# Moving the later loads of a transformer-block backward kernel from the Pool queue to the SP queue

## The chip, the cores and the metric

One core of one Trainium2 chip. The metric is the device time of one execution in microseconds (us). Quoted times are medians of 3 to 7 executions. All executions used below are of the same, undisturbed state except where it is said. The profiled execution has a span about 2 us shorter than its time; spans are compared with spans and times with times. "Granted PE clock" is the share of the matmul engine's full clock that the profile shows as granted, as a mean over the span or a stretch.

The engines appear under the profile's names: PE (matmul), PEld (its weight loads), DVE (vector), ACT (scalar), POOL (GpSimd), SP (sync; here it only issues transfers). Sixteen DMA engines serve all queues of the core.

## The reference

Forward and gradients of `x + attention(layernorm(x)) + ffn(layernorm(x))` for a decode step: batch 4, one query position, D = 512, 32 query heads on 8 key/value heads of 128, a cache of 4096 positions of which only the last 1024 are attended, and a gated FFN of width 1792. Cut to what matters:

```python
def _A_ref(x, k_cache, v_cache, wq, wo):        # W = 1024 of Sk = 4096
    k = jnp.repeat(k_cache[:, :, Sk - W:, :], rep, axis=1)
    v = jnp.repeat(v_cache[:, :, Sk - W:, :], rep, axis=1)
    ...
return x + _A_ref(xn, ...) + _B_ref(xn, ...)
# outputs: the value, and d/d(x, k_cache, v_cache, wq, wo, w_gate, w_up, w_down)
```

The gradients of both caches are outputs in full size. Three quarters of each are zeros, which must still be written: 50 MB of the 81 MB that the kernel writes.

## The kernel before

After the FFN part, four groups (t = 0 to 3, two key/value heads each) pass through the same steps. Group t + 2 is fetched when group t no longer needs its buffers. Everything fetched after the start is issued by `nc.gpsimd` (POOL); all results are stored by `nc.sync` (SP); the zero fills are issued by `nc.scalar` (ACT).

```python
def load_w(t):
    eng = nc.gpsimd if t else nc.sync
    pool = wpool[t % 2]
    wo_t[t] = pool.tile([P, HG, D], BF16, name="wo_sb", tag="wo")
    eng.dma_start(out=wo_t[t][:], in_=wo_v[t])
    wq_t[t] = pool.tile([P, ND, CW], BF16, name="wq_sb", tag="wq")
    eng.dma_start(out=wq_t[t][:], in_=wq_v[t])

def load_kv(t, k, g):
    d_, src, nm = ((k_t, A_k_cache, "kb"), (v_t, A_v_cache, "vb"))[k]
    tl = kvpool[(GP * t + g) % (2 * GP)].tile([P, J, Dh], BF16, name=nm, tag=nm)
    (nc.gpsimd if GP * t + g > GP else nc.sync).dma_start(out=tl[...], in_=src[...])
    ...
def load_next(t):
    if t + 2 < NT:
        load_w(t + 2)
        for k in range(2):
            for g in range(GP):
                load_kv(t + 2, k, g)
...
def zeros(n):                      # n units of 768 KB, at most 4 in one transfer
    ...
        w = min(n, B * G - r, GP * 2)
        z = store(nc.scalar, zdst, zsrc, "zeros", ["rest", "zeros"])
...
# how many units to fill at the four places of each group's score step
ZN = ((0, 4, 4, 4), (0, 4, 4, 2), (2, 4, 4, 4), (4, 4, 4, 4))
```

A scheduler places the issues, so their order on an engine is not always that of the text. And every transfer issued by SP or ACT takes one of eight completion semaphores in turn; an issue waits until the transfer eight places before it has landed. The transfers of POOL have eight of their own. Below, the transfer that took a semaphore last is called its holder.

## Time and profile before

| | before |
|---|---|
| time, median of 3 (range) | 281.89 us (280.82 to 281.97) |
| profiled span, granted PE clock | 279.6 us, 0.888 |
| PE, DVE, ACT, POOL busy | 76%, 57%, 41%, 20% |
| bytes moved by the queues, mean rate over the span | 112.15 MB, 401 GB/s |

No compute engine is near full, and the transfers are: the prediction shows the lines. Two more views of the kernel before are needed for what follows. First, stretches of the windows view (columns: stretch, length; busy us and count for PE, PEld, DVE, ACT, POOL; PE clock; mean busy share of the DMA engines; GB/s), cut where the kernel after will differ:

```profile
100.00:120.00 20.00, 19.13 (x223) 11.12 (x220) 13.42 (x25) 11.26 (x20) 4.64 (x7) 0.91 1.01 419
150.00:170.00 20.00, 16.56 (x222) 10.95 (x221) 11.51 (x20) 9.96 (x18) 7.46 (x10) 1.00 0.99 381
215.00:220.00 5.00, 4.12 (x40) 2.45 (x40) 2.72 (x7) 2.18 (x6) 0.00 (x0) 1.00 1.00 424
```

Second, the last stretches, in the same columns:

```profile
266.00:270.00 4.00, 0.00 (x0) 0.00 (x0) 2.27 (x7) 0.00 (x0) 0.00 (x0) 0.50 1.01 407
270.00:274.00 4.00, 0.00 (x0) 0.00 (x0) 0.00 (x0) 0.00 (x0) 0.00 (x0) 0.50 0.29 114
274.00:278.00 4.00, 0.00 (x0) 0.00 (x0) 0.00 (x0) 0.00 (x0) 0.00 (x0) 0.50 0.06 25
```

The last column but one is the thing to read. From 274 to 278 us the mean share is 0.06, one sixteenth: 25 GB/s, as if one of sixteen engines still had work and fifteen had none. The others ran out between 270 and 273 us.

### The profile page before, as it was taken

What the parts mean: (1) busy time and instruction counts of PE and PEld (TensorE: products, weight loads), DVE (VectorE), ACT (ScalarE), POOL (GpSimd) and SP (SyncE); (2) the same over time, 40 slices, a digit from 0 to 9 for tenths busy, and PEclk for the clock granted to TensorE, in tenths of its full rate; (3) what the DMA queues carried; (4) which work ended last, traced back from release to release, by engine and by line L of the source; (5) the groups of instructions that cost most, each with busy time, mean ns of one, the idle gap of its engine ahead of it and who ended that gap; (6) DMA issues with size and microseconds to landing.
All of it is one profiled execution on the core that took longest, in us unless ns stands there. A gap on an engine that the chain in (4) does not pass through costs nothing.

```text
span 279.6 us, 7185 instructions
## 1 busy us (share of the span) xinstructions
PE 212.1 (76%) x3126; PEld 137.7 (49%) x3132; DVE 158.7 (57%) x336; ACT 115.0 (41%) x214; POOL 56.0 (20%) x56
## 2 busy tenths in 40 slices
PE   1978976988769879968797978699897775689400
PEld 0856854744435565535465745356664442355200
DVE  6955644546357657654665555477654634376530
ACT  1331643444335246636253544373444442525400
POOL 3890003040200345020007600200520020020000
PEclk9985998699797997999689999999999997597955
DMA  7999999999999999999999999999999999999970
GB/s 236 446 392 430 425 403 392 414 411 423 425 426 422 422 423 416 417 432 423 427 418 350 387 407 430 421 425 421 425 415 431 428 422 423 425 432 421 422 311 22
DMA packets 19423, 112.15 MB, mean 401 GB/s; under 512 B 1456, under 2 KB 5056, under 8 KB 10432
## 3 DMA queue, kind: packets, MB, share of 16 engines
q10 hardware_dynamic: 4400, 50.34, 42.7%
q1 hardware_dynamic: 12304, 44.58, 39.3%
q0 software_dynamic: 2688, 16.78, 15.0%
q8 instruction: 24, 0.39, 0.5%
q14 instruction: 7, 0.06, 0.0%
HBM read 30.68 MB, written 81.01 MB: 399 GB/s over the span
## 4 chain that ended last, share of the span: by engine, by line
PE 52%; DVE 19%; DMA 18%; issue 3%; POOL 2%; ACT 2%; ACTq 0%; DVEq 0%
DMA out_dram<-osb_q 13%; PE T_ps L402 9%; PE kv_ps L540 8%; DVE T_sb L101 6%; PE S_ps L407 6%; DMA out_dram<-osb_g 5%; PE woT_ps L339 3%; PE wgT_ps L745 3%; PE acc_ps L213 2%; PE wqT_ps L598 2%; PE dwo_ps L559 2%; POOL P_x L420 2%; PE od_ps L512 2%; PE dwg_ps L718 2%; PE do_ps L344 2%
## 5 line engine op out<-in xcount | busy, mean ns | idle before, releaser
L101 DVE COPY T_sb<-T_ps 128x1024 bf16<-128x1024 bf16 x64 | 43.8, 690 | 40.1 <-PE T_ps L402 39.6
L99 ACT CAST stg_dv<-kv_ps 128x512 bf16<-128x512 f32 x57 | 30.1, 594 | 33.5 <-PE kv_ps L540 25.8
L99 ACT CAST stg_dk<-kv_ps 128x512 bf16<-128x512 f32 x40 | 22.3, 592 | 36.4 <-PE kv_ps L540 22.8
L540 PE MATMUL kv_ps<-domr,P_x 128*128 128x512 bf16 x63 | 23.4, 439 | 10.5 <-ACT stg_dv L99 5.1
L387 POOL TENSOR_TENSOR domr<-r,msk 128x512 bf16<-128x512 bf16 x8 | 8.2, 1040 | 74.1 <-DVE r L380 74.1
L99 ACT CAST osb_g<-dwg_ps 128x512 bf16<-128x512 f32 (+1 forms) x28 | 14.2, 538 | 19.0 <-PE dwg_ps L718 9.2
L402 PE MATMUL T_ps<-ident,kb 128*128 128x128 bf16 x256 | 21.9, 222 | 0.0
L402 PEld LDWEIGHTS <-kb 128*128 128x128 bf16 x256 | 17.1, 100 | 8.6 <-issue 5.7
L540 PE MATMUL kv_ps<-qmr,dS_x 128*128 128x512 bf16 x60 | 20.9, 432 | 0.5 <-DVE stg_dk L101 0.2
L402 PE MATMUL T_ps<-ident,vb 128*128 128x128 bf16 x256 | 20.8, 223 | 0.1
L99 ACT CAST osb_o<-dwo_ps 128x512 bf16<-128x512 f32 x25 | 14.6, 586 | 12.9 <-PE dwo_ps L559 11.8
L402 PEld LDWEIGHTS <-vb 128*128 128x128 bf16 x256 | 16.2, 100 | 6.9 <-issue 5.0
L407 PE MATMUL S_ps<-T_sb,dom 128*32 128x256 bf16 x128 | 12.7, 387 | 8.3 <-DVE T_sb L101 7.8
L420 POOL TENSOR_TENSOR P_x<-P_b,bmsk 128x1024 bf16<-128x1024 bf16 x4 | 7.6, 1893 | 56.2 <-ACT P_b L468 56.2
L99 ACT CAST osb_q<-dwq_ps 128x512 bf16<-128x512 f32 x25 | 14.1, 589 | 11.1 <-PE dwq_ps L571 6.1
L101 DVE CAST stg_dk<-kv_ps 128x512 bf16<-128x512 f32 x24 | 16.0, 684 | 1.8 <-PE kv_ps L540 1.7
L101 DVE COPY woT<-woT_ps 128x1024 bf16<-128x1024 bf16 x16 | 11.0, 689 | 10.0 <-PE woT_ps L339 10.0
L407 PE MATMUL S_ps<-T_sb,qm 128*32 128x256 bf16 x128 | 13.1, 388 | 4.0 <-DVE T_sb L101 4.0
L339 PE MATMUL woT_ps<-ident,wo_sb 128*128 128x128 bf16 x128 | 12.3, 248 | 2.7 <-DVE stg_dv L101 1.9
L101 DVE COPY wgT<-wgT_ps 128x1024 bf16<-128x1024 bf16 x14 | 9.7, 692 | 7.6 <-PE wgT_ps L745 7.6
L339 PEld LDWEIGHTS <-wo_sb 128*128 128x128 bf16 x128 | 10.4, 113 | 7.2 <-issue 6.4
L101 DVE COPY wqT<-wqT_ps 128x1024 bf16<-128x1024 bf16 x16 | 11.0, 687 | 4.7 <-PE wqT_ps L598 4.6
(214 smaller groups left out, 397.4 us busy)
## 6 DMA issues: line engine op xcount, KB each, us to landing
out_dram<-ztile ACTq DMA_DIRECT2D x14, 3072.0 KB, 22.4
out_dram<-stg_dv SPq DMA_DIRECT2D x8, 1024.0 KB, 25.4
out_dram<-stg_dk SPq DMA_DIRECT2D x8, 1024.0 KB, 17.2
out_dram<-ztile ACTq DMA_DIRECT2D x4, 1536.0 KB, 12.7
kb<-in_A_k_cache_dram POOLq DMA_DIRECT2D x5, 1024.0 KB, 20.0
vb<-in_A_v_cache_dram POOLq DMA_DIRECT2D x5, 1024.0 KB, 24.3
out_dram<-osb_o SPq DMA_DIRECT2D x8, 512.0 KB, 15.8
out_dram<-osb_q SPq DMA_DIRECT2D x8, 512.0 KB, 28.1
```

The source lines that it names most:

```text
L99: last.append(nc.scalar.copy(out=out, in_=in_))
L101: return nc.vector.tensor_copy(out=out, in_=in_)
L213: nc.tensor.matmul(ps[:, c, :], lhsT=lf(c), rhs=rhs, start=(k == 0), stop=(k == len(terms) - 1))
L339: nc.tensor.transpose(wT_ps[:, i, c, :], wo_sb[:, 2 * h2 + i, c * P:(c + 1) * P], ident[:])
L344: nc.tensor.matmul(do_ps[i * RG:(i + 1) * RG, 2 * h2:2 * h2 + 2], lhsT=dyT8[:, c, :], rhs=woT[:, :, c, :].rearrange("p j (g x) -> p j g x" ...
L387: nc.gpsimd.tensor_tensor(out=mr[:, g], in0=st[t]["r4"][:, k, :].unsqueeze(1).broadcast_to([P, NQ, Dh]), in1=msk[:, :, g].unsqueeze(2).bro ...
L402: nc.tensor.transpose(T_ps[:, jj, :], blks[(t, g)][:, q * JQ + jj, :], ident[:])
L407: nc.tensor.matmul(ps[b * RG:(b + 1) * RG, :], lhsT=lf[:, b, s * RG:(s + 1) * RG], rhs=T_sb[:, :, b], start=(g == 0 and q == 0), stop=(g = ...
L420: eng.tensor_tensor(out=dst[:].rearrange("p j (m b) -> p (j m) b", b=B), in0=src[:].unsqueeze(2).broadcast_to([P, WQ, B]), in1=bmsk[:].uns ...
L512: nc.tensor.matmul(od_ps[r0:r0 + rep * B, 0, :], lhsT=pT[:, j % JQ, (j // JQ) * GP + g:P:NS], rhs=blks[(t, g)][:, j, :], start=(j == 0), s ...
L540: nc.tensor.matmul(mps[:].rearrange("p q d -> p (q d)"), lhsT=src[:, jj, :], rhs=mr[:, g].rearrange("p q d -> p (q d)"), start=True, stop= ...
L745: nc.tensor.transpose(wT_ps[:, i, c, :], wsb[:, c, fc * P:(fc + 1) * P], ident[:])
```

## The change

The intent: take the 16 later loads (16.78 MB) from POOL's queue and put them into SP's, between the stores; the weights when a group ends, keys and values one at a time in the next group's key steps.

```diff
-    def load_w(t):
-        eng = nc.gpsimd if t else nc.sync
+    loads = deque()
+    def pull(n):
+        for _ in range(min(n, len(loads))):
+            loads.popleft()()
+    def fetch(out, in_, first):
+        d = (nc.sync if first else nc.sync).dma_start(out=out, in_=in_)
+    def load_w(t, k):
         ...                               # wo if k == 0, else wq, each through fetch
     def load_kv(t, k, g):
-        (nc.gpsimd if GP * t + g > GP else nc.sync).dma_start(out=..., in_=...)
+        fetch(..., ..., GP * t + g <= GP)
     def load_next(t):
         if t + 2 < NT:
-            load_w(t + 2)
+            for k in range(2):
+                load_w(t + 2, k)
             for k in range(2):
                 for g in range(GP):
-                    load_kv(t + 2, k, g)
+                    loads.append(lambda k=k, g=g: load_kv(t + 2, k, g))
 ...                                       # in the score step, q counts the blocks
                 tick(2 if k or q % 2 else 1)
+                if k == 0 and q % 2 == 0:
+                    pull(1)
 ...                                       # before the groups
-        load_w(1)
-        for k in range(2):
-            load_kv(1, k, 1)
+        for k in range(2):
+            loads.append(lambda k=k: load_w(1, k))
+        for k in range(2):
+            loads.append(lambda k=k: load_kv(1, k, 1))
```

(Cuts marked with dots.) In the built programs PE, DVE and ACT have the same instructions in the same order before and after. SP's stream has the 16 loads more, POOL's 16 fewer. The scheduler puts group 1's four loads ahead of all eight stores of the FFN weight gradients (`osb_g`), although the text defers them.

More of the change, by code (lines that the diff above doesn't have):

```diff
@@ L275 @@
     kvpool = [kvp] * 3
-    def load_w(t):
-        eng = nc.gpsimd if t else nc.sync
-        pool = wpool[t % 2]
-        wo_t[t] = pool.tile([P, HG, D], BF16, name="wo_sb", tag="wo")
-        eng.dma_start(out=wo_t[t][:], in_=wo_v[t])
-        wq_t[t] = pool.tile([P, ND, CW], BF16, name="wq_sb", tag="wq")
-        eng.dma_start(out=wq_t[t][:], in_=wq_v[t])
+    loads = deque()
[5 more added lines that the diff above has]
+    def load_w(t, k):
+        pool = wpool[t % 2]
+        if k == 0:
+            wo_t[t] = pool.tile([P, HG, D], BF16, name="wo_sb", tag="wo")
+            fetch(wo_t[t][:], wo_v[t], t == 0)
+        else:
+            wq_t[t] = pool.tile([P, ND, CW], BF16, name="wq_sb", tag="wq")
+            fetch(wq_t[t][:], wq_v[t], t == 0)
     def load_kv(t, k, g):
@@ L287, in load_kv @@
         tl = kvpool[(GP * t + g) % (2 * GP)].tile([P, J, Dh], BF16, name=nm, tag=nm)
-        (nc.gpsimd if GP * t + g > GP else nc.sync).dma_start(out=tl[:].rearrange("p j d -> p (j d)"),
-                          in_=src[:, t * GP + g, K0:Sk, :].rearrange("b (m j) d -> m b (j d)", j=J))
+        fetch(tl[:].rearrange("p j d -> p (j d)"),
+             src[:, t * GP + g, K0:Sk, :].rearrange("b (m j) d -> m b (j d)", j=J), GP * t + g <= GP)
         d_[(t, g)] = tl
@@ L613 @@
     NF4 = (NF + 3) // 4
-    load_w(0)
+    for k in range(2):
+        load_w(0, k)
     for k in range(2):
```

## The prediction

> **What bounds the kernel now.** I read the page's DMA rows first, because every engine on the page is well below full (PE 76%, DVE 57%, ACT 41%) while the DMA row is not.
>
> ```profile
> DMA  7999999999999999999999999999999999999970
> GB/s 236 446 392 430 425 403 392 414 411 423 425 426 422 422 423 416 417 432 423 427 418 350 387 407 430 421 425 421 425 415 431 428 422 423 425 432 421 422 311 22
> q10 hardware_dynamic: 4400, 50.34, 42.7%
> q1 hardware_dynamic: 12304, 44.58, 39.3%
> q0 software_dynamic: 2688, 16.78, 15.0%
> ```
>
> The 16 DMA engines are 90% busy or more in 37 of 40 slices. q10 is the zero fill issued by ACT, q1 is SP (first loads, all stores of results), q0 is Pool's loads: 16 of 1 MB, 16.78 MB. Bytes over busy time give the rate of each: q10 50.34 MB in 0.427 x 279.6 us = 422 GB/s, q1 406 GB/s, q0 400 GB/s. So the kernel moves 112 MB at a nearly fixed rate, and what can be won is only the places where the rate drops. The windows view sizes them (columns: stretch, length, then busy us and count of PE, PEld, DVE, ACT, POOL, then PE clock, DMA share, GB/s):
>
> ```profile
> 5.00:40.00 35.00, 28.73 (x541) 23.47 (x542) 23.21 (x71) 12.77 (x20) 12.59 (x8) 0.85 1.03 421
> 40.00:75.00 35.00, 28.28 (x361) 18.18 (x363) 17.86 (x35) 14.64 (x31) 8.54 (x9) 0.88 1.02 408
> 75.00:150.00 75.00, 63.97 (x975) 40.17 (x977) 45.19 (x88) 33.31 (x63) 13.32 (x15) 0.90 1.01 423
> 150.00:157.00 7.00, 5.54 (x104) 4.29 (x104) 3.54 (x7) 3.71 (x7) 3.55 (x6) 1.00 0.95 322
> 157.00:165.00 8.00, 7.10 (x77) 4.27 (x76) 5.32 (x9) 4.10 (x7) 3.91 (x6) 1.00 1.01 405
> 165.00:271.00 106.00, 78.31 (x1071) 47.24 (x1072) 60.30 (x117) 45.21 (x86) 11.61 (x8) 0.91 1.01 422
> 271.00:279.60 8.60, 0.00 (x0) 0.00 (x0) 0.00 (x0) 0.00 (x0) 0.00 (x0) 0.50 0.09 34
> ```
>
> Three dips, all where Pool's loads run. Then the chain that ended last, and the waits, to see where DMA holds the compute:
>
> ```profile
> 56.90 13.97 DMA out_dram<-osb_g
> 226.83 35.79 DMA out_dram<-osb_q
> ACT osb_g L99 <- DMA out_dram<-osb_g: 7.0, 4, 3.6
> ```
>
> The chain is compute up to 57 us, one wait for a store of an FFN gradient tile to land (its buffer is reused), compute again from 71 to 227, and from there the DMA queue itself. Last, the DMA view of the stretch 44 to 56 us, for how three queues share:
>
> ```profile
> q10 hardware_dynamic: 253, 2.97, 62.4%
> q0 software_dynamic: 252, 1.49, 29.7%
> q1 hardware_dynamic: 335, 0.34, 7.9%
> ```
>
> q10 and q0 moved the same number of packets (253 and 252) but twice the bytes, and the store queue, whose rows are 1 to 3.5 KB there, got a fourteenth of the bytes. The queues take turns by packet, so a queue's share of the rate follows its row size.
>
> **What the Trainium skill says.** (1) "DMA: Bandwidth & Descriptors", section "Issuing engines are not separate DMA queues": all issuers share the same 16 engines, and issuing from several only saves sequencer time. The trace agrees as to the rate: 421 GB/s with SP alone (5 to 40 us, almost all q1), 422 with SP and ACT (165 to 271). (2) Same page, "Queues, rings and completion order": each engine goes round the queues packet by packet. The 253 to 252 packets agree. (3) Same page, "Where 436 GB/s comes from": a ceiling of 435 GB/s. The trace sits at 421 to 423, so there is no higher rate waiting. (4) Same page, "Latency and other measured facts": first byte after some 0.6 us for SP and ACT, 1 us for Pool. No line here shows the first byte of one transfer; the landing times (10 to 43 us) are queueing.
>
> **The change part by part.** The listing of the two built programs shows that PE, DVE and ACT run the same instructions in the same order; only SP's stream, Pool's stream and semaphore waits differ.
>
> (a) It removes 16 DMA issues from Pool, 0.53 to 0.77 us each, about 9.5 us of 56 us busy. Pool is 20% busy and 2% of the chain: worth about 0, at most 0.6 us per group where the product od_x stood behind a load (97.79 in the timeline, after the issue at 97.18).
>
> (b) It adds 16 issues of some 0.55 us to SP, about 9 us. SP waits for results nearly all the time: worth 0 unless a load that waits for its buffer holds up a finished store.
>
> (c) The 16.78 MB leave q0 for q1. If the dips are the cost of the software queue, they are recovered: 40 to 75 us, (421 - 408) x 35 = 0.46 MB or 1.1 us at 421; 150 to 157, (423 - 322) x 7 = 0.71 MB or 1.7 us; 157 to 165, 17 x 8 = 0.14 MB or 0.3 us. Sum 3.1 us, 1.1% of 281.9. The other reckoning, q0 at 422 in place of 400, gives 16.78 MB x (1/400 - 1/422) = 2.2 us. That is the whole of what can be won from rate.
>
> (d) Group 1's four loads (4 MB) go into SP's queue at about 44 us, ahead of the eight osb_g stores. Estimate: the 3 MB zero fill on q10 runs till about 52 us with the last 1 KB-row osb_d stores trickling beside it; then SP has the engines alone, 4 MB / 0.42 = 9.8 us, till 62; the first osb_g lands at about 63 us (before, 61.9) and the next ones at 64, 66 and 66 to 70 (before 65.5, 71.0, 76.1), as the ACT waits ended then. So the first release comes 1 us later, the others 1 to 6 us earlier. PE had about 4 us idle between 55 and 75 us; I take a shift of the compute of -1 us, between -3 and +2.
>
> (e) At 150 us the queue runs dry (322 GB/s, q10 has nothing left). Before, Pool issues V at 149.98 and K at 152.44 as soon as group 1 has done with its buffers. In the new SP stream only V stands there; both K loads come behind the weights, which wait for the sums at 156.5, and behind the second dK store at 158. So from about 149 to 157 only V and one dK store are there, 2 MB, against 2.25 MB that moved from 150 to 157 before. Whatever (c) gained up to then (1.1 us) only makes the queue run dry sooner; when it refills is set by compute. In time: the refill comes about 1.5 us after 157, when the old kernel would be 0.25 MB + 1.5 us x 0.42 = 0.9 MB further, that is 2 us; with the 0.3 us of 157 to 165 got back, +1.7 us; with the compute shift of (d), -1, about +0.7 us. If instead the compute before 150 us comes 2 to 3 us sooner, the dip closes and the change wins 1 to 2 us.
>
> (f) All transfers of SP and ACT take completion semaphores in turn from one set of eight, each waiting for its last holder; the Pool loads had eight of their own. With 16 more in the one set, an issue waits for the transfer eight places back. In the listing most of those are 20 us or more old; a few zero fills on ACT wait for a load issued 10 to 16 us before (at 121, 173 and 181 us). One or two such waits of 1 to 3 us on ACT, whose compute has slack there: 0 to +1.5 us.
>
> Sum: (c) up to -3.1, (e) taking most of it back, (d) -1 to +1, (f) +0.5: I put -0.5 us.
>
> **The rivals.** *A: the rate is recovered whole.* Software loads are slow (packets of q0 were 51.9% of the engines' time in 150 to 157 for 1.02 MB, 281 GB/s), and the hardware queue fills the dip. For it: all three dips stand on Pool's loads. Against: 75 to 150 us had six of those loads and ran at 423. Result 279 us. *B: the dip at 150 grows*, as compute, not the queue, refills it and K comes later. For it: the order of SP's stream, and q10 empty from 150 to 157. Against: dK or compute may come sooner. Result 282 to 284. *C: head of line.* A load waiting for its buffer blocks stores; or stores and loads in one queue behind zero fills with larger rows land late, and a group's PE waits for weights or K. For it: loads now share q1's part with stores. Against: group 2's weights are issued at 104 us and needed at 134, K and V at 157, and even five MB at 8 KB rows against 12 KB rows (0.4 of 422, 170 GB/s) take under 30 us, and the zeros do not last that long. Result 285 to 290. *D: nothing*, since queueing hides every issue: 281.9.
>
> **Range and chances.** The middle of A, B and D lies at 281.4 us. A and the best of (d) bound it below at 278.8, B with a semaphore wait above at 284.6. Faster by over 2% needs 5.6 us; the dips hold only 3.1, so that takes a second gain I don't see: 0.03. Slower by over 2% is C: 0.09. Within 2%: 0.88.
>
> **What would show it.** q0 is gone from the queue rows, q1 holds 61 MB; the rate in 5 to 40 and after 165 us stays 420 to 424; 44 to 63 us has the loads on q1 and no dip; the ACT wait for osb_g ends near 63 us and later ones are shorter; a dip at or just before 150 us stays, with q10 empty, at least as deep; DMA ends some 8 us before the span does, as before. I am wrong if PE waits for woT, K or V at a group's start, if SP's waits on a load's buffer delay a finished store by many us, if there is no dip at 150 us, or if the steady rate itself moves off 422.

## The result

| | before | after |
|---|---|---|
| time, median of 4 runs each (range) | 281.93 us (280.82 to 282.18) | 285.04 us (284.37 to 286.31) |
| ratio after/before, 95% interval | | 1.0123 (1.0079 to 1.0168) |
| profiled span, PE clock | 279.6 us, 0.888 | 284.2 us, 0.891 |

A ratio is the mean time of one kernel's fast runs over that of the other's fast runs of the same rounds, so it is not quite the ratio of the medians. The change costs about 3 us: within 2%, but 0.4 us above the predicted range, whose middle lay 0.5 us below the kernel before. The profiled execution of the kernel after was the slowest of its four (286.31 us), so its span, 4.6 us longer than before, overstates the change by about 1.5 us.

The kernel after, the page's rate row in 40 slices and its queue rows:

```profile
GB/s 239 442 398 426 423 395 428 385 394 373 421 419 424 422 381 386 320 427 426 428 414 394 328 314 422 430 424 425 427 410 289 419 434 408 422 421 425 423 417 182
q1 hardware_dynamic: 15760, 61.35, 55.0%
q10 hardware_dynamic: 4400, 50.34, 42.0%
```

The software queue is gone, as wanted, and no rate was won. Bytes over busy time give SP's queue 61.35 MB in 0.550 x 284.2 us, 393 GB/s; before, the same bytes on q1 and q0 took 0.543 x 279.6 us, 404 GB/s. The rate row of before had one deep dip, 350; the row of after has 320, 328, 314 and 289. Sized by the windows view of the kernel after:

```profile
5.00:40.00 35.00, 28.37 (x554) 23.36 (x555) 23.15 (x72) 12.78 (x20) 12.57 (x8) 0.85 1.02 418
40.00:75.00 35.00, 23.10 (x316) 14.54 (x316) 14.79 (x31) 12.59 (x26) 4.04 (x4) 0.85 1.00 396
100.00:120.00 20.00, 16.68 (x216) 10.23 (x206) 11.56 (x21) 9.90 (x18) 5.41 (x5) 0.91 0.99 359
150.00:170.00 20.00, 17.36 (x362) 12.36 (x361) 12.56 (x26) 8.43 (x16) 5.93 (x5) 1.00 0.93 337
215.00:220.00 5.00, 4.71 (x94) 3.80 (x92) 2.77 (x8) 2.17 (x4) 1.64 (x2) 0.88 0.59 246
278.00:284.20 6.20, 0.00 (x0) 0.00 (x0) 0.00 (x0) 0.00 (x0) 0.00 (x0) 0.50 0.38 147
```

Against before (408, 419, 381 and 424 in the four middle stretches), the bytes missing are worth, at 423 GB/s, (408 - 396) x 35 / 423 = 1.0 us, then 2.8, 2.1 and 2.1 us: 8 us of missing work. ("Missing work" is time that the missing bytes would take at the steady rate.) The span grew by 4.6 us only. Two questions follow: what makes the holes, and where did half of their cost go?

**The first hole** starts at 44 us. SP's timeline before, and then after (start, duration, engine, line, transfer):

```profile
43.23 0.37 SPq L105 DMA_DIRECT2D out_dram<-osb_d  x1
46.30 32.69 SPq L105 DMA_DIRECT2D out_dram<-osb_g  x8
```

```profile
42.87 0.37 SPq L105 DMA_DIRECT2D out_dram<-osb_d  x1
43.33 1.25 SPq L284 DMA_DIRECT2D wo_sb<-in_A_wo_dram  x1
44.76 1.13 SPq L284 DMA_DIRECT2D wq_sb<-in_A_wq_dram  x1
45.99 1.44 SPq L284 DMA_DIRECT2D kb<-in_A_k_cache_dram  x1
47.48 1.72 SPq L284 DMA_DIRECT2D vb<-in_A_v_cache_dram  x1
49.31 33.88 SPq L105 DMA_DIRECT2D out_dram<-osb_g  x8
```

Four loads of 1 MB stand before the first `osb_g` store, which goes out 3 us later and, behind their bytes, lands later still. The chain of waits of the kernel after (start, duration, what) and ACT's waits (us in total, times, longest):

```profile
49.31 17.65 DMA out_dram<-osb_g
...
163.77 31.45 DMA kb<-in_A_k_cache_dram
195.24 0.61 ACTq L105
```

```profile
ACT osb_g L99 <- DMA out_dram<-osb_g: 9.8, 1, 9.8
ACT stg_dv L99 <- DMA kb<-in_A_k_cache_dram: 5.9, 1, 5.9
ACT P_b L481 <- DMA out_dram<-stg_dk: 3.6, 1, 3.6
```

The first release shows on ACT's timeline, where the bracket is the idle time before and what ended it; before, and then after:

```profile
61.94 0.59 ACT L99 CAST osb_g<-dwg_ps 128x512 bf16<-128x512 f32 x1 [0.83 <-DMA out_dram<-osb_g]
```

```profile
67.06 0.58 ACT L99 CAST osb_g<-dwg_ps 128x512 bf16<-128x512 f32 x1 [9.76 <-DMA out_dram<-osb_g]
```

So the first `osb_g` lands at 67 us instead of 62, and PE is idle from 60 to 65 us. The row product that ends group 0's attention (`od_r` on DVE) starts at 96.04 us before and at 100.33 us after: the compute runs 4.3 us late, while the queue drains at its own pace. So the queue is thin at 100 to 120 us, and again when group 1 ends, at 150 to 170 us.

Thin is not empty: the share of DMA in these two stretches is 0.99 and 0.93, so the engines were mostly busy and their packets took longer. From 116 to 118 us, for example, the DMA view counts 152 packets of 2.2 KB on average at a share of 0.87; that is 0.87 x 16 x 2 us / 152 = 183 ns each, where 423 GB/s over 16 engines would give 82 ns. Only at 215 to 220 us (share 0.59, 246 of 424 GB/s) did the engines stand idle in proportion to the missing bytes. In what follows a "hole" is a stretch with bytes missing, of either kind; why a packet takes longer when little else is queued, no run tests.

**The last hole** comes from elsewhere. ACT waits 5.9 us before a copy of value gradients, for a key load that this copy does not need. What stands in between is the zero fill that ACT issues at 195.24 us: its completion semaphore was last held by that key load, which took 31.45 us to land. The 3.6 us wait, at the fill of 181.13 us, is of the same kind. (Two such waits exist before too, 4.4 and 3.4 us, but late, at 234 and 239 us.) They hold up the casts that PE waits for: `od_r` of group 2 starts at 209.95 us after, at 196.96 us before, 13 us late where group 1's was 5 us late (153.96 against 148.78). The next zero fills are placed in group 3's steps; they go out at 220.58 and 228.33 us instead of 206.51 and 213.80, and the queue is nearly dry at 218 us (share 0.44 from 217 to 219 us).

**The end.** In the kernel after, the last stretches read

```profile
274.00:278.00 4.00, 0.00 (x0) 0.00 (x0) 0.13 (x1) 0.00 (x0) 0.00 (x0) 0.50 0.99 407
278.00:282.00 4.00, 0.00 (x0) 0.00 (x0) 0.00 (x0) 0.00 (x0) 0.00 (x0) 0.50 0.58 224
282.00:284.00 2.00, 0.00 (x0) 0.00 (x0) 0.00 (x0) 0.00 (x0) 0.00 (x0) 0.50 0.02 8
```

There is no long 0.06 tail any more: all engines run dry nearly together. That is my theory of where half the cost went. One DMA engine lags behind the others; before, it works without a pause until 278 us while the others wait at the end. Every hole lets it catch up, and until it has, holes are free. This is an inference from mean shares, and how far it holds is taken up at the end.

### The profile page after: what moved, and what is told of

Same layout as the page of the kernel before. It is cut to its first block, busy times and chain, and to the rows that moved or that the text cites.

```text
span 284.2 us, 7178 instructions
## 1 busy us (share of the span) xinstructions
PE 210.4 (74%) x3126; PEld 136.6 (48%) x3132; DVE 158.3 (56%) x336; ACT 115.0 (40%) x214; POOL 46.4 (16%) x40
## 3 DMA queue, kind: packets, MB, share of 16 engines
q1 hardware_dynamic: 15760, 61.35, 55.0%
## 4 chain that ended last, share of the span: by engine, by line
PE 50%; DVE 20%; DMA 17%; issue 4%; ACT 3%; POOL 1%; SPq 0%; ACTq 0%; DVEq 0%
DMA kb<-in_A_k_cache_dram 11%; PE kv_ps L553 9%; PE T_ps L413 7%; DMA out_dram<-osb_g 6%; DVE T_sb L101 5%; PE S_ps L418 5%; PE woT_ps L350 3%; PE acc_ps L213 3%; PE dwo_ps L572 3%; PE wqT_ps L611 3%; PE od_ps L525 3%; PE wgT_ps L759 2%; PE do_ps L355 2%; PE dwg_ps L732 1%; PE dwq_ps L584 1%
## 5 line engine op out<-in xcount | busy, mean ns | idle before, releaser
L413 PE MATMUL T_ps<-ident,vb 128*128 128x128 bf16 x256 | 21.7, 228 | 0.1
L553 PE MATMUL kv_ps<-qmr,dS_x 128*128 128x512 bf16 x60 | 19.7, 412 | 1.8 <-DVE dS_x L433 1.4
L350 PEld LDWEIGHTS <-wo_sb 128*128 128x128 bf16 x128 | 10.7, 115 | 10.8 <-issue 10.0
L418 PEld LDWEIGHTS <-qm 128*32 128x32 bf16 x128 | 4.2, 94 | 20.1 <-issue 18.6
```

The lines of the kernel that those rows point to most:

```text
L350: nc.tensor.transpose(wT_ps[:, i, c, :], wo_sb[:, 2 * h2 + i, c * P:(c + 1) * P], ident[:])
L413: nc.tensor.transpose(T_ps[:, jj, :], blks[(t, g)][:, q * JQ + jj, :], ident[:])
L418: nc.tensor.matmul(ps[b * RG:(b + 1) * RG, :], lhsT=lf[:, b, s * RG:(s + 1) * RG], rhs=T_sb[:, :, b], start=(g == 0 and q == 0), stop=(g = ...
L553: nc.tensor.matmul(mps[:].rearrange("p q d -> p (q d)"), lhsT=src[:, jj, :], rhs=mr[:, g].rearrange("p q d -> p (q d)"), start=True, stop= ...
```

## The experiments

The theory has three parts: (1) group 1's loads ahead of `osb_g` delay the compute; (2) the later twelve loads delay zero fills through the shared semaphores and leave keys late; (3) both matter only through holes in the queue that are deeper than the slowest engine's lag. Rivals: the count of holders in the shared semaphores, the deferral, ACT's waits themselves, and a mean-rate view in which each microsecond of hole costs one. In all, 15 kernels ran, each correct; each batch shared runs of the kernel before (281.31 to 281.93 us).

### Group 1's loads back on POOL, the other twelve on SP (g1_pool)

```diff
-        d = (nc.sync if first else nc.sync).dma_start(...)
+        d = (nc.sync if first else nc.gpsimd).dma_start(...)   # first: all but group 1
-            loads.append(lambda k=k: load_w(1, k))              # and load_kv(1, k, 1)
+            load_w(1, k)
```

> The changed kernel, but group 1's four loads are on Pool again, where they were before; the twelve loads of groups 2 and 3 stay on SP. Theory Order (group 1's four loads stand on SP ahead of the eight osb_g stores, so the first osb_g lands at 67 us in place of 62 and all compute after it is 4 to 5 us late): the wait for osb_g is back to about 59 to 62 us, the first od_ps ends near 96 us, and the time is 282 to 283 us. Theory Lanes (the loads share the eight completion semaphores with stores and zero fills, so zero fills hold ACT and SP until a load has landed): the waits of ACT on a K load and on a dK store at 180 to 195 us stay, 284 to 285 us. Theory Hole (K and V issued later leave the DMA queues empty near 105 to 120 and 155 to 170 us): the dips below 380 GB/s at the two group ends stay, 284 to 285 us.

284.24 us, ratio 1.0070 (1.0028 to 1.0112). The early delay is gone: the longest `osb_g` wait is 3.6 us as before, `od_r` starts at 96.75 us. 0.7% remains. ACT's largest wait, and the stretches of 150 and 205 us (before: 366 and 427 GB/s):

```profile
ACT P_b L481 <- DMA out_dram<-stg_dk: 9.8, 1, 9.8
```

```profile
150.00:165.00 15.00, 12.46 (x179) 8.62 (x180) 9.13 (x17) 7.70 (x14) 5.13 (x5) 1.00 0.97 332
205.00:220.00 15.00, 13.99 (x272) 9.98 (x271) 8.70 (x21) 5.84 (x11) 5.92 (x5) 0.89 0.81 331
```

### Group 1's loads on SP, the other twelve on POOL (g1_sp_only)

```diff
-        d = (nc.sync if first else nc.sync).dma_start(...)
+        d = (nc.sync if first else nc.gpsimd).dma_start(...)   # first: groups 0 and 1
-                    loads.append(lambda k=k, g=g: load_kv(t + 2, k, g))
+                    load_kv(t + 2, k, g)
```

> The other half: group 1's four loads on SP ahead of the osb_g stores as in the changed kernel, the twelve later ones on Pool at once when a group ends, as before. Theory Order: the first osb_g lands near 67 us, compute is 4 us late at the first od_ps (100 us), the time 284 to 285 us. Lanes or Hole: the early delay is taken up again because compute has slack there, ACT has no wait on a load after 100 us, the dips are as before, and the time is 282 to 283 us.

285.22 us, ratio 1.0118 (1.0063 to 1.0172): as much as the whole change, though with a wide spread: 285.16 to 286.89 us in the three runs with a granted clock of 0.876, and 283.01 us in the one with 0.905. ACT waits 8.7 us for `osb_g`, and no unrelated wait follows later. Its stretches:

```profile
100.00:120.00 20.00, 16.65 (x182) 10.45 (x181) 10.50 (x19) 8.96 (x16) 8.85 (x11) 0.74 0.97 357
150.00:170.00 20.00, 19.05 (x376) 13.11 (x374) 13.06 (x27) 8.90 (x17) 9.44 (x11) 0.91 0.84 312
205.00:220.00 15.00, 13.63 (x203) 9.09 (x193) 9.53 (x18) 7.32 (x13) 5.76 (x5) 1.00 1.02 423
```

So the early delay alone makes the holes at 100 and 150 us, and does not make the one at 215. Each half of the change alone costs more than half of what the whole costs (0.7% and 1.2% of 1.2%); the two do not add.

### Sixteen tiny loads on SP in the kernel before (before_tiny)

```diff
+    def tiny_load(i):      # 32 bytes, placed where the change places a load
+        d = nc.sync.dma_start(out=tiny[:, i * 4:(i + 1) * 4], in_=A_x...[:, 0:4])
```

> The kernel before, with its loads on Pool, and 16 tiny loads of 32 bytes on SP at the places where the changed kernel has its loads: they take the same completion semaphores in the same turn but move nothing. Theory Lanes: ACT waits at a zero fill for an earlier transfer after 100 us (0 in the kernel before), SP waits more on transfers eight places back (31 us before), and the time goes up by 1.5 to 3 us, to 283.5 to 285. Order or Hole: within 0.7 us of the kernel before, as no bytes have moved.

282.21 us, ratio 1.0015 (0.9993 to 1.0036). Sixteen more holders of the eight shared semaphores cost nothing that shows, at most 0.4%. The number of holders isn't the cost; what can hold an issue up is a holder that lands late, such as the key load of 31 us.

### The text's deferral made real (pinned)

```diff
+        if not first:                  # keep each load behind the last store traced
+            tc.add_manual_dep(d.ins, sp_last[-1].ins.name, ...)
```

> The changed kernel, with each later load tied (order only, no wait) behind the last SP store that stands ahead of it in the program text, so that the scheduler can't draw it forward: group 1's loads go between the osb_g stores. Theory Order: osb_g lands at 60 to 63 us, compute at the first od_ps is no later than before (96 us or earlier), the time 281 to 283 us. Lanes: ACT still waits for a load or store at zero fills after 100 us and the time stays at 284 to 285. Hole: the dips at 105 to 120 and 155 to 170 us stay, since K and V come as late as in the changed kernel, 284 to 285 us.

294.27 us (288.11 to 295.82), profiled slow, so no ratio and the size is not to be compared. In that slow execution the queue is nearly empty for 11 us (share of DMA in the last column but one):

```profile
104.00:109.00 5.00, 4.45 (x58) 3.23 (x57) 3.35 (x6) 2.22 (x4) 0.00 (x0) 0.78 0.02 8
161.00:167.00 6.00, 5.37 (x166) 3.99 (x167) 3.86 (x10) 1.79 (x5) 3.60 (x3) 1.00 0.06 19
```

This suggests that the loads are wanted early, but only a slow execution shows it; the one run in the fast state took 288.11 us. The scheduler had undone most of the deferral in the kernel after.

### SP as issuer, no deferral (sp_immediate)

```diff
-        eng = nc.gpsimd if t else nc.sync
+        eng = nc.sync
-        (nc.gpsimd if GP * t + g > GP else nc.sync).dma_start(...)
+        nc.sync.dma_start(...)
```

> The kernel before with nothing changed but the issuing engine: all sixteen later loads on SP, K and V asked for at once when a group ends and not in the next group's K steps. The built order differs from the changed kernel's only in K and V of groups 2 and 3 standing before the second dK store. Theory Hole: the dips at 110 to 120 and 155 to 170 us are smaller, 283 to 284 us. If the issuing engine is the whole cause and the deferral nothing: 284.5 to 285.5 us, as the changed kernel.

284.51 us, ratio 1.0123 (1.0086 to 1.0159), the ratio of the kernel after. The deferral in the text adds nothing measurable; the issuer accounts for the whole change.

### Group 1's loads issued by ACT (g1_act)

```diff
+            fetch(wo_t[t][:], wo_v[t], t == 0, nc.scalar if t == 1 else None)  # wq, kb, vb too
```

> The changed kernel with group 1's four loads issued by ACT, so that they are hardware-queue loads and take the same eight completion semaphores, but stand in another queue than the osb_g stores. Theory Fifo (the osb_g stores land late because 4 MB of loads stand ahead of them in SP's own queue; not because the loads are hardware-queue loads): the 9.8 us wait of ACT for osb_g goes back to several waits of at most 4 us, the first od_r comes at 96 to 98 us as with group 1 on Pool (96.75), and the time is 283.5 to 284.5 us. If any hardware-queue load does it: od_r at 100 us and 285 us.

284.24 us, ratio 1.0115 (1.0076 to 1.0153). No wait for `osb_g` is left and `od_r` starts at 96.61 us, so it was the order within SP's queue, not the hardware kind of the queue, that delayed the stores. The time does not follow: a wait of 10.7 us at a later zero fill, and 317 GB/s from 205 to 220 us.

### Two zero fills moved from ACT to SP (zeros_sp)

```diff
-                    zeros(ZN[t][GP * k + g])
+                    zeros(ZN[t][GP * k + g], nc.sync if t == 2 and k == 1 else None)
```

> The changed kernel with the two zero fills of group 2's V half issued by SP in place of ACT, so that their wait for a completion semaphore can't hold up ACT's copies and softmax. Theory Lanes, in its refined form (ACT stands 3.6 and 5.9 us at two zero fills in group 2, each waiting for the transfer eight places back, which is a load or store in SP's backlog; the tiny loads showed that the count alone is harmless, 1.0015): these two ACT waits go, the dip at 215 to 220 us (246 GB/s, 2 us lost) closes or halves, and the time falls by 1 to 2.5 us to 282.5 to 284 us. If the ACT waits were hidden anyway, 285 us.

286.31 us, ratio 1.0177 (1.0147 to 1.0207): ACT's waits at these fills are gone, 215 to 220 us runs at 432 GB/s, and it is no faster (the interval overlaps that of the kernel after). SP's waits for zero fills to land rise to 28.8 us in all, from 24.0 in the kernel after. The 317 GB/s from 150 to 170 us are not the edit's doing, since the moved fills go out at 180 and 191 us.

### The same two fills on POOL (zeros_pool)

```diff
+                    zeros(ZN[t][GP * k + g], nc.gpsimd if t == 2 and k == 1 else None)
```

> The kernel after with the two zero fills of group 2's value half issued by Pool, on completion semaphores of their own. Theory (the two waits of ScalarE at its zero fills, 3.6 and 5.9 us in the kernel after, are on the path): both waits are gone and the time falls to about 283 to 284 us. Rival (holes in the queue alone count, the waits are slack): the waits are gone and the time stays at 285.

285.97 us, ratio 1.0154 (1.0106 to 1.0202). All that is left of ACT's long waits on transfers is the early one:

```profile
ACT osb_g L99 <- DMA out_dram<-osb_g: 8.7, 1, 8.7
ACT osb_q L99 <- DMA out_dram<-osb_q: 0.9, 1, 0.9
```

```profile
150.00:170.00 20.00, 18.76 (x375) 13.09 (x375) 12.69 (x26) 9.16 (x17) 5.92 (x5) 0.91 0.89 316
208.00:220.00 12.00, 10.08 (x153) 6.77 (x153) 6.89 (x13) 5.62 (x10) 3.06 (x4) 1.00 1.02 421
```

ACT's waits had been my favourite cause, and this speaks against them: neither ACT nor SP is held at those fills, `od_r` of group 2 follows that of group 1 after 48.5 us (56.0 in the kernel after), the hole at 215 us is closed, and the kernel is no faster; the intervals overlap. The hole at 150 us is deeper (316 against 337 in the kernel after), but not through the edit: up to 180 us SP and ACT issue the same transfers in the same order in both. This execution, the slowest of its four, had a lower granted clock just before (the kernel after, then this one; the clock is the last column but two):

```profile
100.00:155.00 55.00, 45.64 (x660) 28.28 (x652) 32.15 (x62) 24.66 (x46) 9.10 (x8) 0.91 1.01 399
100.00:155.00 55.00, 46.37 (x572) 28.83 (x575) 31.48 (x60) 24.68 (x46) 7.08 (x6) 0.84 1.01 396
```

### One zero fill moved into the hole, kernel before (fill_150)

```diff
-    ZN = (..., (2, 4, 4, 4), (4, 4, 4, 4))
+    ZN = (..., (0, 4, 4, 4), (4, 4, 4, 4))
+            zeros(2 if t == 1 else 0)      # at about 142 us
```

> The kernel before with one 1.5 MB zero fill drawn forward from the start of group 2 (159.6 us) to the end of group 1 (about 146 us). Theory Empty queue (time is lost wherever nothing is left in the queues, and compute sets when they fill again): the dip of 322 GB/s from 150 to 157 us closes, and the time falls by 0.7 to 1.7 us to 280.3 to 281.3 us. If the software loads themselves are slow, the dip stays and nothing changes.

281.12 us, ratio 0.9996 (0.9970 to 1.0023). 150 to 157 us now runs at 402 GB/s instead of 322, worth (402 - 322) x 7 / 423 = 1.3 us, and no gain shows:

```profile
266.00:270.00 4.00, 0.00 (x0) 0.00 (x0) 0.00 (x0) 0.00 (x0) 0.00 (x0) 0.50 0.70 277
270.00:274.00 4.00, 0.00 (x0) 0.00 (x0) 0.00 (x0) 0.00 (x0) 0.00 (x0) 0.50 0.07 30
274.00:278.00 4.00, 0.00 (x0) 0.00 (x0) 0.00 (x0) 0.00 (x0) 0.00 (x0) 0.50 0.06 23
```

Set beside the same three lines of before: the others finish over 1 us sooner, the straggler still at 278 us. This dip of the kernel before was mostly or wholly free; the interval leaves room for a gain of 0.8 us.

### The same move in the kernel after (after_fill)

Edit as in fill_150.

> The kernel after with that one zero fill moved forward, nothing else. If the hole at 150 to 170 us (three slices under 380 GB/s) is on the path in the kernel after: 283.5 to 284.3 us. If it is covered, as it was in the kernel before: 285, no difference.

283.90 us, ratio 1.0068 (1.0024 to 1.0111), where the kernel after had 1.0123. Here the same edit pays about half of the loss, though the two intervals overlap. It closes two holes, since the shifted fills also take other semaphores (ACT's only long wait on a transfer left is 7.0 us for `osb_g`):

```profile
150.00:170.00 20.00, 17.13 (x349) 12.18 (x348) 11.38 (x24) 7.97 (x16) 5.96 (x5) 0.91 1.02 420
215.00:220.00 5.00, 4.27 (x47) 2.46 (x47) 2.93 (x5) 1.75 (x3) 0.00 (x0) 1.00 1.03 424
```

### Group 1 on POOL and more (g1_zpool, g1_zpool_fill, g1_fill)

g1_zpool joins the edits of g1_pool and zeros_pool; g1_zpool_fill adds the moved fill; g1_fill is g1_pool with the moved fill and all fills on ACT.

> The same, and group 1's four loads back on Pool, so that neither the early delay of osb_g nor the waits at the zero fills is left. Theory (these two are all that the change costs): 282 to 282.7 us, within 0.4% of before. Rival (the holes in the queue around 150 to 170 us and 215 us are a third cost by themselves): 283.5 to 284.5, as with group 1 on Pool alone.

283.36 us, ratio 1.0051 (1.0028 to 1.0075).

> The same, and one 1.5 MB zero fill at about 142 us in place of 160 us, into the hole at 150 to 165 us. If that hole costs time in this version: 0.5 to 1 us below the version without it, 281.5 to 282. If the slowest transfer engine still has work through it: no difference.

283.08 us, ratio 1.0040 (1.0018 to 1.0061).

> Group 1's loads on Pool, the other twelve on SP, and the 1.5 MB zero fill at about 142 us in place of 160 us; all zero fills still issued by ScalarE. If the hole at 150 to 165 us is the cause of what group 1 on Pool left over (284.24 us): 283 us, as with the zero fills on Pool as well. If the waits of ScalarE at its fills matter beside it: 284.

282.98 us, ratio 1.0054 (1.0013 to 1.0094). In g1_fill ACT waits as long as in any of them, and it is no slower than g1_zpool_fill, where no wait of ACT for a transfer exceeds 3 us:

```profile
ACT P_b L481 <- DMA wq_sb<-in_A_wq_dram: 8.8, 1, 8.8
```

```profile
205.00:220.00 15.00, 14.16 (x216) 9.53 (x205) 8.89 (x18) 6.73 (x12) 5.92 (x5) 0.89 0.75 308
```

So an 8.8 us wait of ACT and a hole worth (427 - 308) x 15 / 423 = 4.2 us made no difference that shows, once the holes at 100 and 150 us were small (403 and 396 GB/s in g1_fill). With the twelve later loads on SP, this is the fastest that I reached: about half a per cent slower than before.

### Holes of known size in the kernel before (hole1, hole2)

```diff
-    ZN = ((0, 4, 4, 4), (0, 4, 4, 2), (2, 4, 4, 4), ...)
+    ZN = ((0, 4, 4, 4), (0, 4, 1, 1), (2, 8, 4, 4), ...)    # hole1; up to 8 units in one transfer
+    ZN = ((0, 4, 4, 4), (0, 1, 1, 1), (2, 8, 7, 4), ...)    # hole2
```

> The kernel before, with the loads on Pool, and 1.5 MB (3.6 us at 423 GB/s) of the zero fills of 122 and 131 us moved behind the hole at 150 us, so that this hole grows from about 1 us to about 4.6 us. Theory (one of the 16 transfer engines lags by some 7 us at the end, so about 4 us at 150 us, and holes shorter than its lag are free): no more than 0.8 us longer than before. Rival (every microsecond of hole costs one): 3 to 3.6 us longer, 285 us.

284.66 us (284.15 to 288.20), ratio 1.0101 (1.0070 to 1.0132).

> The same with 2.6 MB (6.2 us) moved, so a hole of about 7 us at 150 us. Theory: about 4 us of it are covered by the lagging engine, 2 to 3.5 us longer than before, 284 to 285.3 us, and the engines end within 3 to 5 us of each other in place of 8. Rival (every microsecond costs one): 6 us longer, 288 us.

291.50 us, ratio 1.0355 (1.0317 to 1.0394).

Both expectations carry an error of mine: a unit is 768 KB, not half of that, so the moved fills were 3.1 and 5.5 MB, 7.4 and 13.0 us at 423 GB/s. With the right sizes the rival expects +7.4 and +13 us, the theory some 4 us less. Measured by time: +3.3 and +10.2 us, so 4.1 and 2.8 us less than the rival. The long tail that the theory wants to see shortened is still there in hole1:

```profile
278.00:282.00 4.00, 0.00 (x0) 0.00 (x0) 0.00 (x0) 0.00 (x0) 0.00 (x0) 0.50 0.47 184
282.00:286.00 4.00, 0.00 (x0) 0.00 (x0) 0.00 (x0) 0.00 (x0) 0.00 (x0) 0.50 0.05 18
```

Hole2's stretch, where before had 388 GB/s:

```profile
135.00:155.00 20.00, 19.11 (x372) 13.11 (x373) 13.17 (x28) 8.71 (x17) 6.16 (x7) 0.84 0.38 150
```

POOL issues all later loads here and PE was no less busy than before (19.1 of 20 us against 17.1), so a starved queue makes such a loss with no later load on SP at all. (ACT waits 6.5 and 14.7 us at fills in these two, so they aren't free of that companion; g1_fill and zeros_pool are what tells it apart.)

### All kernels beside one another

For each profiled execution: the rate from 5 to 150 and from 150 to 270 us in the windows view; the work missing against before, which is ((419 - first) x 145 + (416 - second) x 120) / 423; and the growth of the span over 279.6 us.

| kernel | GB/s 5-150, 150-270 | work missing, us | span longer, us | free, us |
|---|---|---|---|---|
| fill_150 | 421, 417 | -1.0 | -0.5 | -0.5 |
| g1_zpool_fill | 418, 416 | 0.3 | 1.5 | -1.2 |
| before_tiny | 415, 414 | 1.9 | 1.2 | 0.7 |
| g1_zpool | 414, 412 | 2.8 | 2.4 | 0.4 |
| after_fill | 405, 420 | 3.7 | 3.2 | 0.5 |
| g1_fill | 416, 404 | 4.4 | 1.8 | 2.6 |
| g1_pool | 413, 400 | 6.6 | 4.0 | 2.6 |
| g1_act | 412, 401 | 6.7 | 3.0 | 3.7 |
| sp_immediate | 409, 404 | 6.8 | 2.6 | 4.2 |
| zeros_sp | 406, 406 | 7.3 | 4.8 | 2.5 |
| g1_sp_only | 406, 405 | 7.6 | 5.5 | 2.1 |
| zeros_pool | 404, 406 | 8.0 | 6.4 | 1.6 |
| hole1 | 401, 409 | 8.2 | 6.8 | 1.4 |
| after | 406, 401 | 8.7 | 4.6 | 4.1 |
| hole2 | 385, 417 | 11.4 | 9.6 | 1.8 |

One execution each, and a rate rounded to 1 GB/s is worth 0.2 us, so single differences under 1 us say little. Hole1's profiled run was its slowest (288.2 us). The span follows the missing work, less 0 to 4 us (g1_zpool_fill excepted). It is not one to one and not independent; the discount tends to be large where a part of the missing work lies after 205 us (after, sp_immediate, g1_act), and small where it lies in one deep hole at 150 us (zeros_pool, hole1, hole2). Pinned is left out, since it was profiled slow.

One companion was not held fixed: the granted clock. In several kernels the executions with the lower clock were the slower ones: zeros_pool took 284.94, 285.23, 286.70 and 287.93 us at 0.908, 0.899, 0.888 and 0.881. It doesn't explain the change itself, as its mean is 0.897 in the four runs of the kernel after and 0.895 in the 28 runs of before that the experiments shared. It may be part of the loss of g1_sp_only (mean 0.883, before in the same rounds 0.893), g1_zpool_fill (0.877, 0.890), hole1 (0.885, 0.901) and hole2 (0.877, 0.901). No run tests it.

## Why the prediction was right or wrong

**The sum.** The -0.5 us is a judgement and not a sum: the shift of (d) enters twice, in (e)'s +0.7 and as a term of its own, where its range of -3 to +2 has become -1 to +1.

**(a) and (b), the issues themselves: nothing speaks against them, with one exception.** No run isolates POOL's freed time; the kernel got slower with it. No finished store is seen held up by a load that waits for its buffer: group 1's first key-gradient store goes out 2.4 us after `od_r` in both kernels. On SP an issue was put at 0.55 us; group 1's four took 1.25, 1.13, 1.44 and 1.72 us. That belongs to (d).

**(c), dips worth 3.1 us: wrong.** Two ways. The rate did not recover when the software queue went (404 to 393 GB/s for the same bytes), so the dips were not the price of that queue. And the dip at 150 us, priced at 1.7 us, was worth at most 0.8: fill_150 closed it and gained 0.04% (up to 0.3%). The step treated the queue as one pipe with a mean rate; on the reading above, the end is set by the engine that finishes last, and that one was working through the dip. The sign was in the tail lines of before.

**(d), group 1's loads ahead of `osb_g`: the mechanism right, the size wrong, and this is the main miss.** Put at a first landing near 63 us and a shift of -1 us, between -3 and +2. It measured 67 us and +4.3 us. The reckoning let SP's four loads have the engines alone from 52 us at full rate and the stores land right after them. The loads went nearly so: SP's queue moved 3.77 MB from 52 to 62 us and 0.79 MB from 62 to 64 us, so their 4.2 MB were through near 63 us, by estimate. But the first store, issued at 49.31 us behind slow issues, landed 17.65 us later, some 4 us behind the loads and not 1 us; what held it in those 4 us stays open. Nor did the later stores repay it: the one wait of 9.8 us replaced four of 7.0 in all. g1_sp_only shows this part alone at +1.2%, as much as the whole change.

**(e), the dip at 150 us stays and grows: right.** 381 became 337 GB/s in 150 to 170 us, 2.1 us of work against the 2 us reckoned; the 1 us that (e) took off for compute coming sooner did not come. And the delay of compute feeds it as much as the order of the keys: g1_sp_only, with those keys on POOL, has 312 there.

**(f), the shared semaphores: the mechanism right, mis-sized at first sight, and then not where it was put.** Predicted: one or two waits of 1 to 3 us on ACT, +0.5. Measured: 5.9 and 3.6 us. Group 2 ends some 8 us later still, which makes the hole at 215 us; zeros_pool, without these waits, does not have it. But zeros_pool is no faster, and g1_fill, with a wait of 8.8 us, no slower than its like without: no cost of such a wait shows in these runs. The prediction had no step from a late issue to a dry queue.

**The rivals.** The outcome is B ("the dip grows, 282 to 284") with more holes than one, and part of C (stores behind loads), which was given 0.09 and looked for at the weights of group 2 rather than at the stores. The steady rate outside the holes stayed at 418 to 424 GB/s, nearly as said; PE did not wait for keys or values, and for `woT` never more than 0.8 us at once. The forecast that DMA ends 8 us before the span, as before, failed.

**Why not worse.** Of 8.7 us of missing work 4.1 us vanished from the span, in step with the loss of the long 0.06 tail. That one lagging engine absorbs it is the reading that fits fill_150 and the two tails; it was inferred from mean shares, since the views do not list the engines one by one. The two runs made to size it fit only in part: by their profiles 1.4 and 1.8 us of the missing work were free, where the theory had about 4, and hole1 keeps a tail. Nor does any run tell an engine that is slower from one that has more to move: the page of before gives the instruction queue q8 0.5% of the engines' span, 0.005 x 16 x 279.6 = 22 us of one engine's time, and on which engines it ran is not shown.

**What stays open.** g1_zpool_fill delivers its bytes as before (0.3 us missing) and is still 0.4% (0.18 to 0.61) slower. It has a short dip at 208 to 212 us (310 GB/s), and its straggler ends about as before; I have no run that tells whether the 1 us is there, behind the last store, or in its lower clock. And the discount of 0 to 4 us is described, not derived.

## What to carry to other kernels

When the DMA engines are the bound, ask of every reordering not what it costs the issuing engine but whether the queue still has work 50 to 100 us later: here a store that went out 3 us late, at 49 us, shifted the compute that refills the queue at 100 and at 150 us. Don't put loads ahead of stores whose buffers are waited for, in one queue, and look at the last lines of the DMA share before pricing a dip: a tail at one sixteenth suggests that a single engine sets the end and that shallow dips may be free. Close one, as fill_150 does, before counting on either. Deferring a load in the text proves nothing until the built order is read.

## What the Trainium skill lacked or had wrong

- "DMA: Bandwidth & Descriptors", section "Issuing engines are not separate DMA queues": that issuing from several engines doesn't add bandwidth holds here (404 GB/s with POOL and SP, 393 with SP alone). What it lacks is that the choice still matters for order: with the same 16 loads on SP the kernel took 1.2% longer, and moving only group 1's to ACT removed the 9.8 us wait for the stores behind them.
- Same page, section "Queues, rings and completion order": it says that each engine takes a ring's descriptors in ring order. The trace agrees, and the consequence could stand there with a number: four 1 MB loads ahead of a store made the first store land at 67.0 instead of 61.9 us.
- Same page, section "Latency and other measured facts", row "DMA engines 7/15": it says that two engines are usually slower and calls it specific to software queues as a best guess. Here a tail of about one sixteenth share lasts from 273 to 278 us in the kernel before. The version after_fill, with no load on POOL, still has a share of 0.06 to 0.08 from 277 to 281 us, so some lag is there without software queues. Which engine it is, and whether it is slower or has more to move, no run here shows.
- No page that I found gives a number for what such a lag costs a kernel bound by transfers. Here closing a dip of 1.3 us gained 0.04% (-0.2 to 0.3%), while 11.4 us of missing work lengthened the span by 9.6 us.
